# Attention with top-k and a mixture of experts on one core: two tiles of x turned by TensorE instead of by DMA

## The chip, the cores and the metric

The kernel runs on one core of a Trainium2 chip, in one launch. The metric is the device time in microseconds (us) of one execution. Five engines work side by side, each on its own list of instructions in order: TensorE (PE, matrix products), VectorE (DVE), ScalarE (ACT), GpSimd (POOL), and SyncE (SP), whose list here holds DMA issues only.

## The reference

Two batches, eight heads, 576 rows of queries and keys, 64 values a head. Attention keeps the 32 largest scores of each row; its output, one row of 512 values for each of 1152 rows, goes through four experts, each a product with w1, a ReLU and a product with w2, weighted by normalised probabilities.

```python
scores = scale * np.matmul(q, k.transpose(0, 1, 3, 2))
kth = np.partition(scores, -32, axis=-1)[..., -32:-31]
scores = np.where(scores >= kth, scores, -1e9)
attn = np.exp(scores - np.max(scores, axis=-1, keepdims=True))
attn = attn / (np.sum(attn, axis=-1, keepdims=True) + 1e-09)
x = np.matmul(attn, v)            # heads side by side: 1152 x 512
p = domain_probs / (domain_probs.sum(-1, keepdims=True) + 1e-09)
for e in range(4):
    h = np.maximum(x @ w1[e], 0.0)
    out += p[:, e:e + 1] * (h @ w2[e])
```

## The kernel before

**Tiles and units.** The 1152 rows are cut into ten tiles: of each batch four of 128 rows and one of 64. The half tile of the first batch comes first (here t0), then its four whole tiles (t1 the first of them), then the second batch. A unit is one head of a whole tile, or a pair of heads of a half tile, so 128 rows of 576 scores: units 0 to 3 are t0, 4 to 11 are t1, and so on to 71.

**Attention of a unit.** PE writes the scores into one of two score banks (L681; L636 for t0). DVE finds the 32 largest in four rounds of MAX8 (L694) with three MATCH_REPLACE8 between them (L696 for the first, L698). ACT takes the exp (L738). The mask sets all below the 32nd to zero: in the early units one DVE operation (L745), later one on ACT (L748) and POOL (L755). The mask reads the scores last, so only then is their bank free. In whole tiles ACT rounds the weights to fp16 (L764), POOL subtracts for the rest (L766, L768), and a DMA transpose on SP (L774) turns both; in t0 PE turns them in fp32 and ACT copies them out (L603, L604). PE multiplies with v (L805; L658 and L661 for t0). The keys are split in the same way, a POOL subtraction for each pair of heads, and turned by DMA transposes (L1141, tiles kt0 to kt7).

**x.** When four heads of a tile are summed, DVE divides them by their totals into x (L823, L825, L827, L829), 256 columns at a time. `emit_x_end` then rounds x to fp16 on ACT (L849, xhl), lets POOL subtract for the rest (L854), and turns both with one DMA transpose on SP (L857) into xt, which holds x turned, high and low parts, as the expert products want it. For t0, `emit_x_whole` turns x also in fp32 on PE (L838) and copies it out (L841), for the two experts whose weights are not yet split.

**Experts.** For each expert and each half of the 1024 hidden columns: first product (L922 to L924, three fp16 products of high and low parts; L897 in fp32), ReLU and split (L933, L940, L947 or L943), second product (L969; L960 in fp32), evacuation times the probability: ACT and POOL (L1014, L1019) or DVE alone (L1016). Weights are loaded by SP (L364), measured by a gram on PE (L528) whose diagonal DVE sums (L534) and PE adds up (L537), scaled by ACT (L558), rounded (L564), and their rest subtracted by POOL (L567).

**What sets the order.** Nothing is scheduled on the chip. Each step is a function, often a generator with several parts, entered with `at(...)`; `events` is drained in the order of the numbers in the table `ISSUE`, one tuple a step, one number a part, and each part's instructions are appended to the lists of their engines. An engine takes its list in order, so an instruction that waits holds back all behind it. Waits between engines follow from tiles written and read.

Of the kernel before, what the change touches and what calls it, by code (L numbers as in the profile page):

```python
# [8 lines left out]
F16 = mybir.dt.float16  # L9
# [37 lines left out]
NB = 'aaaaddddddaddaadaddddpdpdadppadpapppaaapppppadaappdaaaaaaapapaaaaaapapaa'  # L47
# [8 lines left out]
PC = ('pppp', 'pppp')  # L56

EVAC = ('ddpp', 'dppp', 'dppp', 'ddpd', 'dppp', 'dpdp', 'dddd', 'dddd', 'dddd', 'dddd')
# [177 lines left out]
def attn_moe_kernel(tc, q, k, v, probs, w1, w2, out):  # L236
# [69 lines left out]
    with tc.manual_schedule(engines={getattr(mybir.EngineType, x) for x in MANUAL}):  # L306
# [451 lines left out]
        def emit_a(u):  # L758
            if units[u][0] == tiles[0]:
                yield from emit_a_whole(u)  # L760
                return
# [8 lines left out]
        def emit_at(u):  # L770
            if units[u][0] == tiles[0]:
                return
# [529 lines left out]
```

## Time and profile before

| | |
|---|---|
| runs of the kernel before | 533.17, 534.58, 536.81 us (median 534.58) |
| profiled execution | 534.99 us, of which the span from first to last instruction is 533.2 us |
| busy in the span | PE 506.3, DVE 432.3, ACT 371.7, POOL 368.8 us |
| weight loads of PE | 377.8 us, beside the matmuls |
| mean granted clock of TensorE | 0.986 of full |

Busy time is an average over stages: PE's 95% does not say where the other 5% are, and DVE's 81% is nearly 100% in one half of the span and almost nothing at its end. A wait is put down to the releaser that came last; "idle before" in a row is the time in which the engine had nothing running ahead of that instruction.

### The profile page before, as it was taken

The page shows a single profiled execution, that of the slowest core. Times are in us where ns is not written, and L with a number is a line of the kernel's source. Part 1 is how long each engine was busy: PE and PEld are TensorE (multiplying, and loading weights), DVE is VectorE, ACT ScalarE, POOL GpSimd, SP SyncE. Part 2 cuts the span into 40 slices and gives each one's busy share as a digit, 9 for nine tenths or more (in the row PEclk, how much of TensorE's full clock was granted, in tenths as well). Part 3 has the DMA queues.
Part 4 walks back from the last instruction along what each step waited for, and adds up shares of the span by engine and source line. Part 5 has one row for each costly group of instructions (what it writes and reads, how often), then busy time and mean ns, then how long its engine had stood idle before and what let it go on. Part 6 is the DMA issues. An engine that isn't in the chain of part 4 may idle for free.

```text
span 533.2 us, 16075 instructions
## 1 busy us (share of the span) xinstructions
PE 506.3 (95%) x6594; PEld 377.8 (71%) x6594; DVE 432.3 (81%) x929; ACT 371.7 (70%) x612; POOL 368.8 (69%) x430
## 2 busy tenths in 40 slices
PE   7787788889999999999999999999999999999996
PEld 6576736477777777877777777777777866778576
DVE  4998989999999999999999999997879856910111
ACT  3899989998889887797777767775655644644121
POOL 0589989999999878678787875875565375454211
PEclk9996989999999999999999999999999999999999
DMA  8999969753465447457654652254232134221100
GB/s 189 316 295 358 219 183 234 164 87 55 90 110 121 103 95 116 94 115 114 125 120 70 97 104 59 57 95 76 57 64 57 30 75 54 21 47 43 33 23 11
DMA packets 142745, 58.33 MB, mean 109 GB/s; under 512 B 130064, under 2 KB 134416, under 8 KB 142672
## 3 DMA queue, kind: packets, MB, share of 16 engines
q1 hardware_dynamic: 138976, 54.43, 49.6%
q10 hardware_dynamic: 3696, 2.88, 1.8%
q8 instruction: 51, 0.84, 0.7%
q14 instruction: 22, 0.18, 0.1%
HBM read 25.45 MB, written 2.36 MB: 52 GB/s over the span
## 4 chain that ended last, share of the span: by engine, by line
PE 74%; DVE 16%; ACT 3%; POOL 3%; DMA 2%; issue 2%; SPq 0%; ACTq 0%; POOLq 0%
PE m L969 30%; PE m L922 10%; PE m L924 10%; PE m L923 10%; DVE m L694 7%; PE av L805 5%; PE ps L681 5%; DVE w L698 3%; DVE w L696 2%; POOL w L567 2%; DMA kraw<-in_k_dram 2%; DVE w L745 2%; PE m L528 1%; ACT w L564 1%; PE av L658 1%
## 5 line engine op out<-in xcount | busy, mean ns | idle before, releaser
L924 PE MATMUL m<-xt,w 128*128 128x128 f16 (+1 forms) x1216 | 191.2, 215 | 0.0
L969 PE MATMUL m<-w,h 128*128 128x512 f16 (+1 forms) x864 | 184.2, 379 | 0.1
L922 PE MATMUL m<-xt,w 128*128 128x128 f16 (+1 forms) x1056 | 171.0, 215 | 0.0
L923 PE MATMUL m<-xt,w 128*128 128x128 f16 (+1 forms) x1056 | 171.0, 215 | 0.0
L694 DVE MAX8 m<-w 128x8 f32<-128x576 f32 x216 | 161.9, 756 | 3.5
L969 PEld LDWEIGHTS <-h 128*128 128x128 f16 (+1 forms) x864 | 78.5, 99 | 85.9 <-DVE h L943 0.6
L924 PEld LDWEIGHTS <-w 128*128 128x128 f16 x1216 | 117.0, 98 | 0.0
L698 DVE MATCH_REPLACE8 w<-m,w 128x576 f32<-128x576 f32 x144 | 107.1, 744 | 0.0
L922 PEld LDWEIGHTS <-w 128*128 128x128 f16 x1056 | 101.9, 98 | 1.8 <-issue 0.4
L923 PEld LDWEIGHTS <-w 128*128 128x128 f16 x1056 | 101.8, 98 | 1.3
L947 POOL TENSOR_TENSOR h<-hf,h 128x512 f16<-128x512 f32 x55 | 63.7, 1159 | 53.8 <-ACT hf L940 29.1
L766 POOL TENSOR_TENSOR a<-w,a 128x512 f16<-128x512 f32 x68 | 78.9, 1160 | 17.6 <-ACT a L764 13.4
L755 POOL TENSOR_TENSOR w<-w,d 128x576 f32<-128x576 f32 x49 | 62.7, 1282 | 37.8 <-ACT d L752 27.8
L738 ACT ACTIVATE w<-ps,nb,es 128x576 f32<-128x576 f32 x68 | 56.3, 828 | 26.0 <-DVE m L694 23.7
L694 DVE MAX8 m<-ps 128x8 f32<-128x576 f32 x72 | 54.4, 756 | 16.2 <-PE ps L681 9.6
L764 ACT ACTIVATE a<-w 128x576 f16<-128x576 f32 x68 | 45.9, 679 | 22.7 <-POOL w L755 16.9
L933 ACT ACTIVATE h<-m 128x512 f16<-128x512 f32 x70 | 41.1, 591 | 23.8 <-PE m L924 23.1
L696 DVE MATCH_REPLACE8 w<-m,ps 128x576 f32<-128x576 f32 x72 | 53.9, 749 | 0.0
L1016 DVE SCALAR_TENSOR_TENSOR o<-m,pniw,o 128x512 f32<-128x512 f32 (+1 forms) x13 | 9.6, 742 | 48.7 <-PE m L969 23.0
L748 ACT ACTIVATE d<-ps,m 128x576 f32<-128x576 f32 x49 | 36.2, 739 | 18.2 <-DVE m L694 13.2
L940 ACT ACTIVATE hf<-m 128x512 f32<-128x512 f32 x55 | 32.5, 590 | 14.9 <-PE m L924 11.7
L805 PEld LDWEIGHTS <-at 128*128 128x128 f16 (+1 forms) x1008 | 35.1, 100 | 8.2 <-issue 4.7
(180 smaller groups left out, 818.5 us busy)
## 6 DMA issues: line engine op xcount, KB each, us to landing
w<-in_moe_w_dram SPq DMA_DIRECT2D x16, 1024.0 KB, 8.0
qraw<-in_q_dram SPq DMA_DIRECT2D x8, 256.0 KB, 4.0
qb<-qa SPq DMA_DIRECT2D x16, 128.0 KB, 3.7
out_dram<-o ACTq DMA_DIRECT2D x8, 256.0 KB, 2.2
at<-a SPq DMA_TRANSPOSE x68, 3.3
vraw<-in_v_dram SPq DMA_DIRECT2D x2, 512.0 KB, 8.3
nraw<-in_v_dram SPq DMA_DIRECT2D x4, 256.0 KB, 3.4
kraw<-in_k_dram SPq DMA_DIRECT2D x4, 256.0 KB, 2.9
```

The costliest lines, as they stand in the source:

```text
L694: DVE.max(m, s_t[u] if r == 0 else w_t[u])
L696: DVE.match_replace(rows2(w_t[u]), m, s_t[u], NEG)
L698: DVE.match_replace(w_t[u], m, w_t[u], NEG)
L738: ACT.activation(rows2(w_t[u]), s_t[u], AF.Exp, bias=nb, scale=es)
L755: POOL.tensor_tensor(w, w, g, op=OP.mult)
L766: POOL.tensor_tensor(a[:, 640:1152], w[:, 0:512], a[:, 0:512], op=OP.subtract)
L805: PE.matmul(o, lhsT=att[:, blk, ps], rhs=r, start=(i == 0), stop=(i == len(seq) - 1))
L922: PE.matmul(o, lhsT=HI[e, 0, c][:, fc], rhs=xs(0, c), start=(c == 0), stop=False)
L923: PE.matmul(o, lhsT=HI[e, 0, c][:, fc], rhs=xs(1, c), start=False, stop=False)
L924: PE.matmul(o, lhsT=LO[e, 0, c][:, fc], rhs=xs(0, c), start=False, stop=(c == 3))
L947: POOL.tensor_tensor(h[:, 1], hf, h[:, 0], op=OP.subtract)
L969: PE.matmul(y[z * 64:z * 64 + M, :], lhsT=h_t[es, qd][:, p // 2, h0:h0 + M], rhs=w, start=(fc == 0 and p == 0), stop=(fc == 7 and p == 2))
```

## The change

For the tiles listed in `X_TURN` (t0 and t1) x is no longer rounded, subtracted and sent through a DMA transpose. PE turns x in fp32 into a PSUM bank by products with the identity, ACT copies the bank to the high part in fp16, and DVE subtracts the high part from the bank for the low part. For t0 the turned x that `emit_x_whole` makes anyway is used, so no transposes are added there; for t1 `emit_x_turned` turns each half of x as soon as it stands. `emit_x_end` is not called for the two tiles. `A_TURN`, for the same with attention weights, is empty, and the function it would call (left out below) issues nothing. One evacuation goes from ACT and POOL to DVE (`EVAC`), one coefficient from POOL to DVE (`PC`), one bias from POOL to ACT (`NB`). The table `ISSUE` is new throughout; its first lines stand for it.

```diff
-NB = 'aaaaddddddaddaadaddddpdpdadppadpapppaaapppppadaappdaaaaaaapapaaaaaapapaa'
+NB = 'aaaaddddddaddaadaddddadpdadppadpapppaaapppppadaappdaaaaaaapapaaaaaapapaa'
-PC = ('pppp', 'pppp')
+PC = ('pppp', 'pppd')
+
+X_TURN = (0, 1)
+A_TURN = ()
-EVAC = ('ddpp', 'dppp', 'dppp', 'ddpd', 'dppp', 'dpdp', 'dddd', 'dddd', 'dddd', 'dddd')
+EVAC = ('ddpp', 'dppp', 'dppp', 'dddd', 'dppp', 'dpdp', 'dddd', 'dddd', 'dddd', 'dddd')
...
 ISSUE = [
-    (15,), (20,), (12,), (65,), (2, 3), (4, 5), (16, 19), (13, 14), (21, 27), (33,), (34, 37), (38, 43, 49, 74),
...
+        def emit_x_turned(t, half):
+            p = bank(ps_m1, "m1")[:, 0:256]
+            for c in range(2):
+                PE.transpose(p[:, c * 128:c * 128 + 128], x_t[t][:, half * 256 + c * 128:half * 256 + c * 128 + 128], ident)
+            yield
+            if half == 0:
+                xT_t[t] = xtp.tile([128, 8, 128], F16, tag="xt", name="xt")
+            hi, lo = (xT_t[t][:, i:i + 2].rearrange("p c n -> p (c n)") for i in (2 * half, 4 + 2 * half))
+            ACT.activation(hi, p, AF.Copy)
+            yield
+            DVE.tensor_tensor(lo, p, hi, op=OP.subtract)
+
         def emit_x_whole(t):
             p = bank(ps_m1, "m1")
             n = 256 if t[2] == 64 else 512
             for c in range(n // 128):
                 PE.transpose(p[:, c * 128:c * 128 + 128], x_t[t][:, c * 128:c * 128 + 128], ident)
+            if 0 in X_TURN:
+                yield
+                xT_t[t] = xtp.tile([128, 8, 128], F16, tag="xt", name="xt")
+                hi, lo = (xT_t[t][:, i:i + 2].rearrange("p c n -> p (c n)") for i in (0, 2))
+                ACT.activation(hi, p[:, 0:n], AF.Copy)
+                yield
+                DVE.tensor_tensor(lo, p[:, 0:n], hi, op=OP.subtract)
             yield
             xF[t] = hfp.tile([128, 512], F32, tag="hf", name="xf")[:, 0:n]
...
                 at(i + P["xh" + early], emit_x_half, t, (u - first_of[t]) // 4)
+                if ti and ti in X_TURN:
+                    at(i + P["xh" + early] + 1, emit_x_turned, t, (u - first_of[t]) // 4)
             if u == last_of[t]:
                 sfx = "_last" if ti == NT - 1 else early
-                emit_x_end(t, ti, [i + P[x + sfx] for x in ("sq", "tot", "hi", "lo")])
-                if t == tiles[0] and F32E:
+                if ti not in X_TURN:
+                    emit_x_end(t, ti, [i + P[x + sfx] for x in ("sq", "tot", "hi", "lo")])
+                if t == tiles[0]:
                     at(i + P["tot_first"], emit_x_whole, t)
```

**How the order moves, first place: DVE between the scores of unit 5 and of unit 6.** The w with the lower number is unit 4's in the first list, the higher one unit 5's; `ps0` in a MAX8 is a fresh bank of scores, here unit 6's, and L823 (L849 of the changed file) reads the sums of unit 3. Before:

```order
L823 TENSOR_SCALAR r_693<-av_471,ix_114 128x4
L694 MAX m_579<-w_605 128x8
L827 RECIPROCAL r_693<-r_693 128x4
L734 TENSOR_SCALAR nb_697<-m_579,es_559 128x1
L698 MATCH_REPLACE w_646<-m_639,w_646 128x576
L829 TENSOR_TENSOR x_692<-av_471,r_693 128x256
L694 MAX m_639<-w_646 128x8
L745 SCALAR_TENSOR_TENSOR w_605<-ps0_567,m_579,w_605 128x576
L698 MATCH_REPLACE w_646<-m_639,w_646 128x576
L694 MAX m_764<-ps0_759 128x8
L694 MAX m_639<-w_646 128x8
```

With the change:

```order
L698 MAX m_645<-w_653 128x8
L698 MAX m_584<-w_618 128x8
L702 MATCH_REPLACE w_653<-m_645,w_653 128x576
L849 TENSOR_SCALAR r_706<-av_482,ix_114 128x4
L698 MAX m_645<-w_653 128x8
L749 SCALAR_TENSOR_TENSOR w_618<-ps0_571,m_584,w_618 128x576
L538 SCALAR_TENSOR_TENSOR m1_710,gd_743<-m1_710,ident_111 128x128
L702 MATCH_REPLACE w_653<-m_645,w_653 128x576
L853 RECIPROCAL r_706<-r_706 128x4
L738 TENSOR_SCALAR nb_751<-m_645,es_611 128x1
L698 MAX m_759<-ps0_754 128x8
```

L823 went behind two more top-k operations; the division (L829, now L855) went behind unit 6's first MAX8, and the sum of the gram's diagonal (L534, now L538), which stood three rows below the first list, went ahead of it.

**Second place: SP's DMA issues from the load of w01 on.** `kt` are turned keys, `w` the raw weights of expert and layer, `khl0` and `xhl` the split keys and x. Before:

```order
L364 DMA w01_124<-in_moe_w2_dram 128x4x512
L1141 DMA_TRANSPOSE kt1_132<-khl0_144 128x5x128
L364 DMA w01_124<-in_moe_w2_dram 128x4x512
L1141 DMA_TRANSPOSE kt3_134<-khl0_144 128x5x128
L1141 DMA_TRANSPOSE kt2_133<-khl0_144 128x5x128
L1141 DMA_TRANSPOSE kt6_137<-khl0_144 128x5x128
L364 DMA w20_127<-in_moe_w1_dram 128x2x1024 x2
L364 DMA w11_126<-in_moe_w2_dram 128x4x512 x2
L1141 DMA_TRANSPOSE kt4_135<-khl0_144 128x5x128
L1141 DMA_TRANSPOSE kt5_136<-khl0_144 128x5x128
L857 DMA_TRANSPOSE xt_907<-xhl_741 128x4x128
L1141 DMA_TRANSPOSE kt7_138<-khl0_144 128x5x128
```

With the change:

```order
L368 DMA w01_124<-in_moe_w2_dram 128x4x512
L1186 DMA_TRANSPOSE kt2_133<-khl0_144 128x5x128
L368 DMA w01_124<-in_moe_w2_dram 128x4x512
L368 DMA w11_126<-in_moe_w2_dram 128x4x512
L368 DMA w20_127<-in_moe_w1_dram 128x2x1024
L1186 DMA_TRANSPOSE kt3_134<-khl0_144 128x5x128
L368 DMA w20_127<-in_moe_w1_dram 128x2x1024
L1186 DMA_TRANSPOSE kt7_138<-khl0_144 128x5x128
L368 DMA w11_126<-in_moe_w2_dram 128x4x512
L1186 DMA_TRANSPOSE kt6_137<-khl0_144 128x5x128
L1186 DMA_TRANSPOSE kt4_135<-khl0_144 128x5x128
L1186 DMA_TRANSPOSE kt5_136<-khl0_144 128x5x128
```

The transpose of xhl is gone, and of the four loads of w11 and w20, which went out together, the later half of each stands behind a key transpose (kt3, kt7). On POOL the subtraction for kt3 and kt7 went from the second of four key subtractions in a row to a place between the first two weight subtractions of w10.

**Third place: DVE just ahead of the scores of unit 16.** L745 (now L749) with `ps0_1593` (now `ps0_1590`) is the mask of unit 12, whose bank unit 16's scores take. Before:

```order
L694 MAX m_1598<-w_1631 128x8
L694 MAX m_1700<-ps0_1693 128x8
L298 TENSOR_SCALAR ws_117<-wpt_1407 128x1
L696 MATCH_REPLACE w_1742<-m_1700,ps0_1693 128x576
L745 SCALAR_TENSOR_TENSOR w_1631<-ps0_1593,m_1598,w_1631 128x576
L694 MAX m_1700<-w_1742 128x8
L534 SCALAR_TENSOR_TENSOR m1_1706,gd_1757<-m1_1706,ident_111 128x128
L698 MATCH_REPLACE w_1742<-m_1700,w_1742 128x576
L295 TENSOR_SCALAR wpt_1761<-m1_1706 128x1
L734 TENSOR_SCALAR nb_1764<-m_1700,es_1191 128x1
```

With the change:

```order
L855 TENSOR_TENSOR x_1437<-av_1558,r_1658 128x256
L702 MATCH_REPLACE w_1614<-m_1611,w_1614 128x576
L870 TENSOR_TENSOR xt_1546<-m1_1542,xt_1546 128x256
L698 MAX m_1611<-w_1614 128x8
L698 MAX m_1702<-ps0_1697 128x8
L870 TENSOR_TENSOR xt_1546<-m1_1693,xt_1546 128x256
L700 MATCH_REPLACE w_1715<-m_1702,ps0_1697 128x576
L538 SCALAR_TENSOR_TENSOR m1_1720,gd_1753<-m1_1720,ident_111 128x128
L698 MAX m_1702<-w_1715 128x8
L749 SCALAR_TENSOR_TENSOR w_1614<-ps0_1590,m_1611,w_1614 128x576
```

The two subtractions of t1 (L870 of the changed file) are new, L534 (now L538) went from behind this mask to ahead of it, and the mask of unit 14 went ahead of the division of x, out of this list.

## Rows read from the trace of the kernel before

**Rows 1.** Windows by stage; columns: stretch, us, busy us (instructions) by engine, PEclk, DMA, GB/s.
```profile
core 0: us, PE busy (x) PEld busy (x) DVE busy (x) ACT busy (x) POOL busy (x), PEclk, DMA share, GB/s
0.00:40.00 40.00, 31.68 (x378) 24.65 (x380) 31.83 (x81) 29.32 (x47) 19.07 (x30) 1.00 1.02 267
40.00:80.00 40.00, 32.12 (x424) 22.87 (x420) 35.86 (x88) 36.41 (x43) 35.98 (x34) 0.83 0.88 253
80.00:111.00 31.00, 25.95 (x300) 16.11 (x297) 30.72 (x77) 29.28 (x35) 30.43 (x32) 1.00 0.88 179
111.00:160.00 49.00, 47.39 (x644) 36.73 (x642) 48.62 (x105) 43.95 (x67) 47.73 (x49) 1.00 0.53 88
160.00:370.00 210.00, 209.99 (x2623) 158.27 (x2621) 202.03 (x421) 158.61 (x294) 160.35 (x206) 1.00 0.53 98
```

**Rows 2.** Timeline of PE: start us, us, engine, line, operation [idle before, what ended it].
```profile
39.76 0.69 PE L658 MATMUL av<-vraw,at 128*64 128x64 f32 x16 [0.53 <-ACT at L603]
...
41.94 3.59 PE L528 MATMUL m<-w 128*128 128x128 bf16 x32
45.33 0.63 PE L838 MATMUL m<-ident,x 128*128 128x128 f32 x2
...
105.98 0.30 PE L681 MATMUL ps<-kt,qa 128*128 128x288 f16 x1 [0.91 <-DVE w L745]
...
106.48 2.00 PE L528 MATMUL m<-w 128*128 128x128 bf16 x32
110.08 0.38 PE L537 MATMUL m<-gd,ones 128*128 128x1 f32 x2 [1.60 <-DVE m L534]
...
110.81 0.22 PE L922 MATMUL m<-xt,wx 128*128 128x128 f16 x1
...
154.86 0.28 PE L681 MATMUL ps<-kt,qa 128*128 128x288 f16 x1 [0.64 <-ACT w L738]
```

**Rows 3.** Timeline of DVE, 40 to 47 us.
```profile
42.05 0.22 DVE L823 TENSOR_SCALAR r<-av,ix 128x4 f32<-128x4 f32 x1 [1.20 <-PE av L661]
...
43.76 0.42 DVE L829 TENSOR_TENSOR x<-av,r 128x256 f32<-128x256 f32 x1
44.09 0.76 DVE L694 MAX8 m<-w 128x8 f32<-128x576 f32 x1
...
46.96 0.77 DVE L694 MAX8 m<-ps 128x8 f32<-128x576 f32 x1 [0.67 <-PE ps L681]
```

**Rows 4.** Timeline of ACT, 38 to 47 us.
```profile
39.13 0.58 ACT L603 ACTIVATE at<-m 128x512 f32<-128x512 f32 x1
...
41.80 1.06 ACT L564 ACTIVATE w<-w 128x1024 f16<-128x1024 f32 x1
```

**Rows 5.** Timeline of DVE, 108 to 110 us.
```profile
108.29 0.81 DVE L745 SCALAR_TENSOR_TENSOR w<-ps,m,w 128x576 f32<-128x576 f32 x1
...
109.68 0.28 DVE L534 SCALAR_TENSOR_TENSOR m<-m,ident 128x128 f32<-128x128 f32 x1
```

**Rows 6.** Timeline of SP, the queue of DMA issues.
```profile
37.91 2.86 SPq L364 DMA_DIRECT2D w<-in_moe_w_dram  x4
...
106.84 1.26 SPq L857 DMA_TRANSPOSE xt<-xhl  x1
```

**Rows 7.** Tile xt: time from issue to landing of its transposes.
```profile
DMA to landing us min/median/max: 2.4/3.4/4.8
```

**Rows 8.** Line 364, weight loads issued from 37 to 41 us: time to landing.
```profile
DMA to landing us min/median/max: 5.9/8.7/12.0
```

**Rows 9.** Window of 42 to 44 us, columns as in rows 1.
```profile
42.00:44.00 2.00, 2.00 (x21) 2.00 (x21) 1.95 (x7) 1.69 (x2) 1.65 (x2) 0.50 1.02 410
```

**Rows 10.** Tile x: duration ns min/median/max, first and last start us, forms.
```profile
L849 ACT ACTIVATE xhl<-x x10: 416/629/631, 44.2 to 500.1; 128x512 f16<-128x512 f32 x8, 128x256 f16<-128x256 f32 x2
L854 POOL TENSOR_TENSOR xhl<-x,xhl x10: 670/1155/1180, 47.7 to 500.6; 128x512 f16<-128x512 f32 x8, 128x256 f16<-128x256 f32 x2
```

**Rows 11.** Line 1016, columns as in rows 10.
```profile
L1016 DVE SCALAR_TENSOR_TENSOR o<-m,pniw,o x13: 732/742/751, 246.3 to 518.9; 128x512 f32<-128x512 f32 x12, 64x512 f32<-64x512 f32 x1
```

More of the change, by code (lines that the diff above doesn't have):

```diff
@@ L756, in emit_mask, with emit_a_turned @@
                 s_give(("d", u))
+        def emit_a_turned(u):
+            t, x = units[u]
+            w = w_t.pop(u)
+            p0 = bank(ps_m1, "m1")
+            if (t, x // 4) not in av_t:
+                av_t[t, x // 4] = bank(ps_av, "av")
+            p1 = av_t[t, x // 4][:, 384:512]
+            for c in range(4):
+                PE.transpose(p0[:, c * 128:c * 128 + 128], w[:, c * 128:c * 128 + 128], ident)
+            PE.transpose(p1, w[:, 448:576], ident)
+            PE.transpose(p1[0:64], w[:, 512:576], ident)
+            yield
+            at_t[u] = tt = atp.tile([128, 9, 128], F16, tag="at", name="at")
+            ACT.activation(tt[:, 0:4].rearrange("p c n -> p (c n)"), p0, AF.Copy)
+            ACT.activation(tt[:, 4], p1, AF.Copy)
+            yield
+            DVE.tensor_tensor(tt[:, 5:9].rearrange("p c n -> p (c n)"), p0, tt[:, 0:4].rearrange("p c n -> p (c n)"), op=OP.subtract)
+            DVE.tensor_tensor(tt[64:128, 4], p1[64:128], tt[64:128, 4], op=OP.subtract)
         def emit_a(u):
@@ L760, in emit_a @@
                 yield from emit_a_whole(u)
+                return
+            if u in A_TURN:
+                yield from emit_a_turned(u)
                 return
@@ L770, in emit_at @@
         def emit_at(u):
-            if units[u][0] == tiles[0]:
+            if units[u][0] == tiles[0] or u in A_TURN:
                 return
@@ L838, in emit_x_whole @@
                 PE.transpose(p[:, c * 128:c * 128 + 128], x_t[t][:, c * 128:c * 128 + 128], ident)
+            if 0 in X_TURN:
+                yield
+                xT_t[t] = xtp.tile([128, 8, 128], F16, tag="xt", name="xt")
+                hi, lo = (xT_t[t][:, i:i + 2].rearrange("p c n -> p (c n)") for i in (0, 2))
+                ACT.activation(hi, p[:, 0:n], AF.Copy)
+                yield
+                DVE.tensor_tensor(lo, p[:, 0:n], hi, op=OP.subtract)
             yield
```

318 rows, old and new, of the table ISSUE are left out of this document.

## The prediction

> **What bounds the kernel now.** I read the table by stages first [rows 1]. TensorE (PE) is busy without a gap from 160 to 370 us and has 1.61 us of idle from 111 to 160 (49.00 - 47.39). Ahead of that it idles 7.88 us from 40 to 80 and 5.05 us from 80 to 111, and there VectorE (DVE) is the full one: 30.72 of 31.00 us from 80 to 111. The reader should see two regimes: up to about 111 us the top-k on DVE hands out the score banks and PE waits for it; from there on PE has expert matmuls in stock and is the bound to the end. So the time is "when PE gets its stock" plus PE's work after that. The second view is PE's own order of time [rows 2]. The stock arrives at 110.81, where the first matmul of the first whole tile (t1) starts. It does not start on x: PE stands first at a gram sum (1.60 us of idle up to 110.08, until DVE's L534 is done) and then at the scores of unit 16, and only behind those come the t1 matmuls. The third view is DVE from 108 to 110 us [rows 5]: the mask of unit 12, a MAX8 between, then the L534 for which PE stood.
>
> The DMA transpose that the change removes had its turn: issued at 106.84 [rows 6], with a median landing of 3.4 us [rows 7] it is there at 110.2, against 110.81. It is hidden by 0.6 us in the median, and at the longest landing of this tile name, 4.8 us, it would be 0.8 us late. So removing it is worth 0 to 0.8 us, and I take 0, because PE names L534 and not a DMA as what it waited for. What the transposes did elsewhere has to pay for the change.
>
> **The change part by part, against the profiled run: 534.99 us with a span of 533.2, 0.41 above the median of the three runs (534.58).**
>
> The extra DVE work. Three subtractions that read PSUM, 128x256 each, come onto DVE ahead of unit 16's scores: one for the half tile t0, two for t1. Otherwise DVE's list up to that point holds the same operations as before. The nearest row is L829, 128x256 out of PSUM: 0.42 us, and the next operation starts 0.33 us after it [rows 3]. Three cost 1.0 to 1.3 us on an engine that is full; **+1.0**.
>
> The stretch from 40 to 47 us. DVE idles 1.20 us for the attention sums of unit 3 and then 0.67 us for the scores of unit 6 [rows 3]. In the new order the L823 on those sums stands two top-k operations later, so the first gap can close; the second is set by PE: sums of unit 3, gram of w01, scores of unit 6, in this order. PE loses 0.53 us ahead of unit 3's sums, waiting for the copy L603 [rows 2], which begins at 39.13 [rows 4]; in the new order one L564 copy (1.06 us [rows 4]) stands behind it instead of ahead. And the two transposes of x (0.63 us [rows 2]) no longer stand between gram and scores. That brings unit 6 about 1.0 us forward. The L534 for w01 now stands ahead of unit 6's first MAX8 and makes DVE wait for the end of the gram, which keeps the gain from being more. **-1.0**, bounds 0 and -1.9 (both DVE gaps).
>
> The order just ahead of the stock. Before, DVE ran mask, MAX8, L534 (from 108.29 to past 109.68 [rows 5]), and PE took the sum and then the scores. Now it runs L534, MAX8, mask: the sum is no longer waited for, and the scores of unit 16 are released by the last of the same three. Nothing is won but the sum's own turn, part of its 0.38 us [rows 2], **-0.2**. Queued behind that wait are unit 16's scores and all of t1's matmuls.
>
> TensorE's new work. Four more transposes of 128x128 fp32. At half clock two take 0.63 us [rows 2]; so four are 0.6 to 1.3 us. The second pair stands ahead of unit 15's scores, where PE idled 0.91 us (at 105.98); the first pair stands in a stretch with 5.05 us of idle. **0** while that cover holds, +1.3 if it doesn't.
>
> ScalarE and POOL. ACT loses an x copy of 0.42 us and one of 0.63 us [rows 10], and gains three of 128x256 out of PSUM, for which the 0.42 us one is the nearest row: +0.2 beside other work, nothing. POOL loses 0.67 and 1.15 us [rows 10]; it is full from 80 to 160 (30.43 of 31.00, 47.73 of 49.00 [rows 1]). Of PE's 1.61 us of idle after 111 the largest piece, 0.64 us before 154.86, ends on an exp on ACT [rows 2]; the ACT chain there runs behind POOL's. I take that one piece as gone, **-0.6**; ends 0 and -1.6.
>
> The rest. One evacuation of the fourth tile goes from ACT and POOL to DVE at 0.74 us [rows 11]; it falls in 160 to 370, where DVE idles 7.97 us against PE's 0.01 [rows 1]: 0. One bias of a single column goes from POOL to ACT and one coefficient from POOL to DVE, 0. After 111 the order of expert matmuls, sums and scores is shuffled by a place or two with the same work: 0. SP loses two transposes and gets its weight loads in another order; that is a rival below.
>
> Sum: 1.0 - 1.0 - 0.2 - 0.6 = -0.8, so 534.99 - 0.8 = **534.2 us**.
>
> [...]
>
> **Rivals.**
>
> *All DVE gaps close* (chance 0.2). Against the forecast, DVE idles 4.14 us from 40 to 80 and 0.28 us from 80 to 111 [rows 1]. If the new order closes these, and PE's 1.61 us after 111 as well, the time is 534.99 + 1.0 - 0.2 - 4.4 - 1.6 = 529.8; with about half of it, 532. For it: two of the gaps are waits for PE at half clock, and a full clock alone would give the gram's 1.6 us back. [...]
>
> *TensorE falls to half clock near 105 us* (chance 0.08). The second pair stands between fp32 matmuls and a gram. If the clock falls there, the gram and what follows cost twice: 1.6 us for the gram, and then PE is already the bound, so the t1 matmuls pay in full. All falls from 40 to 80 us together cost 40 x (1 - 0.83) = 6.8 us of full clock [rows 1]; half of that, 3.4, for one fall here. 534.2 + 3.4 = 537.6, slower than before. It decides if the granted clock falls below 1 between 105 and 115 us.
>
> *The second halves of w20 and w11 come late* (chance 0.15). Before, four loads went out together at 37.91 [rows 6] and landed 5.9 to 12.0 us later, median 8.7 [rows 8]. Now the second half of each stands on SP behind a key transpose (kt3, kt7), and kt3 waits for POOL's key subtraction, which has moved behind a weight subtraction. By POOL's pace that is near 41 us; the loads would go out near 44 and 46, and at 8.7 us land near 52.5 and 55. The grams of w20 and w11 stand in PE ahead of unit 8's scores, so DVE then starves with them: about +1.9 us at the median, +5.2 at 12.0 us. The time is 536.1, and 539.4 at the worst. For it: nothing else can slip in between, PE is in order. Against it: with fewer loads at a time each should land sooner. It decides if the later half lands after 53 us.
>
> *The turn does nothing that counts* is the forecast's own core: neither removed transpose ended last.
>
> **How the numbers follow.** Forecast and its neighbourhood (533 to 536) 0.52; gaps close (529.8 to 533) 0.2; late weights (536 to 539.4) 0.15; half clock 0.08 (near 537.6); 0.05 for a wait that I don't see in the shuffled stages. The range 530.0 to 538.5 leaves out the far ends of these, under 2 in 10. A measurement of this kernel tells about 1%, 5.3 us, from no change: faster than 529.2 needs every gap gone and a little more, 0.08; slower than 539.9 needs the longest landings or two mishaps together, 0.08; the rest, 0.84, is within 1%.
>
> **What would show it.** The first t1 matmul starts at 110.0 to 111.0 us; no idle of 1.6 us before the gram sum just ahead of it; DVE's idle from 40 to 80 near 3 us instead of 4.14, and its idle at 42 us gone, with a wait of up to 1 us for the gram of w01 in its place; PE idle from 111 to 160 near 1 us; granted clock 1.00 from 80 us on. The forecast is wrong if the first t1 matmul starts before 108 or after 113 us, if PE idles in 160 to 470, or if the grams of w20 and w11 wait for a DMA.

## The result and the profile of the changed kernel

The changed kernel takes 539.67 us (median of six runs; 538.17 to 540.02), the kernel before 534.97 us beside it (six runs, 533.17 to 536.81). The ratio that goes with these runs is 1.0068 with the interval 1.0044 to 1.0092; it is not the quotient of the two medians, which is 1.0088. The forecast was 534.2 us, a little faster, in a range of 530.0 to 538.5 us: the kernel became slower, and the time lies above the range. The profiled execution has a span of 538.1 us, 4.9 longer than before. One run of old_order_behind_16 below (1034.43 us) and one of the kernel before beside it (542.63 us) were slow ones, and the figures here leave them out.

The windows by stage, with the columns of [rows 1]:

```profile
0.00:40.00 40.00, 32.24 (x330) 23.99 (x330) 29.18 (x76) 27.48 (x46) 16.56 (x28) 0.97 1.04 277
40.00:80.00 40.00, 32.66 (x441) 25.06 (x442) 35.46 (x85) 33.37 (x38) 33.27 (x30) 0.74 0.82 223
80.00:111.00 31.00, 27.41 (x311) 16.66 (x306) 30.90 (x77) 29.28 (x40) 30.29 (x34) 1.00 0.80 178
111.00:160.00 49.00, 45.84 (x612) 35.90 (x610) 48.39 (x109) 46.16 (x67) 47.52 (x47) 1.00 0.51 93
160.00:370.00 210.00, 209.47 (x2593) 156.56 (x2592) 201.98 (x419) 158.38 (x294) 158.79 (x201) 1.00 0.52 96
```

Against [rows 1], DVE has done 2.65 us less work in the first 40 us (29.18 for 31.83), ahead of the stretch from 40 us that the prediction costed; the granted clock from 40 to 80 fell from 0.83 to 0.74; and PE idles 0.53 us from 160 to 370, where it had idled 0.01.

The timeline of PE in the same kernel, columns as in [rows 2]; L640 is the scores of unit 0, L648 the weight transposes of unit 3, L685 scores, L662 attention sums, L532 grams:

```profile
8.49 1.88 PE L640 MATMUL ps<-kf,qf 64*64 64x288 f32 x8
...
37.24 1.11 PE L648 MATMUL m<-ident,w 128*128 128x128 f32 x4 [0.86 <-DVE w L749]
...
38.93 0.42 PE L685 MATMUL ps<-kt,qa 128*128 128x288 f16 x1
...
40.01 1.12 PE L662 MATMUL av<-vraw,at 128*64 128x64 f32 x16
...
45.44 3.59 PE L532 MATMUL m<-w 128*128 128x128 bf16 x32
48.83 0.44 PE L685 MATMUL ps<-kt,qa 128*128 128x288 f16 x1
...
54.12 0.42 PE L685 MATMUL ps<-kt,qa 128*128 128x288 f16 x1 [3.91 <-DVE wpt L299]
```

The same places in the kernel before (L636 is the scores of unit 0, L681 those of unit 5, L644 the weight transposes of unit 3):

```profile
7.48 1.19 PE L636 MATMUL ps<-kf,qf 64*64 64x288 f32 x8
...
35.93 0.28 PE L681 MATMUL ps<-kt,qa 128*128 128x288 f16 x1
...
36.42 0.60 PE L644 MATMUL m<-ident,w 128*128 128x128 f32 x4
```

Two things differ. In the durations, from 37.24 us on matmuls take half as long again to nearly twice as long as the same ones at full clock (16 sums in 1.12 us for the 0.69 of [rows 2]): the granted clock from 37 to 58 us is 0.51, near the 0.50 of [rows 9], and was 0.76 before. The first row is the same at the start: 8 score matmuls in 1.88 us, where before they took 1.19. In the order, the scores of unit 5 stood ahead of unit 3's transposes and now stand behind them and behind their wait. What DVE makes of it, columns as in [rows 3]:

```profile
10.41 0.77 DVE L698 MAX8 m<-ps 128x8 f32<-128x576 f32 x1 [2.33 <-PE ps L640]
...
40.11 0.77 DVE L698 MAX8 m<-ps 128x8 f32<-128x576 f32 x1 [1.40 <-PE ps L685]
...
45.56 0.22 DVE L849 TENSOR_SCALAR r<-av,ix 128x4 f32<-128x4 f32 x1 [0.52 <-PE av L665]
...
49.07 0.30 DVE L538 SCALAR_TENSOR_TENSOR m<-m,ident 128x128 f32<-128x128 f32 x1 [1.90 <-PE m L532]
...
110.66 0.41 DVE L870 TENSOR_TENSOR xt<-m,xt 128x256 f16<-128x256 f32 x1
```

Between the first MAX8 of unit 4 and that of unit 6, three waits for PE, 3.82 us in all, stand where two stood before with 1.87 us [rows 3]; DVE's own work there is the same (11.53 us, before 11.54). The last row is one of the new subtractions. Unit by unit, the first MAX8 is later than in the profile before ("late" in what follows) by 1.70 us (unit 0), 0.99 (unit 3), 1.29 (unit 4), 2.79 (unit 5), 3.24 (unit 6), and 3.43 (unit 16): only 0.19 us are added between units 6 and 16. The first expert matmul of t1 starts 3.14 us late, at 113.95. Then PE:

```profile
112.11 0.38 PE L541 MATMUL m<-gd,ones 128*128 128x1 f32 x2 [0.64 <-DVE m L538]
113.45 0.30 PE L685 MATMUL ps<-kt,qa 128*128 128x288 f16 x1 [0.95 <-DVE w L749]
...
113.95 0.22 PE L967 MATMUL m<-xt,w 128*128 128x128 f16 x1
...
120.14 0.30 PE L685 MATMUL ps<-kt,qa 128*128 128x288 f16 x1 [0.67 <-DVE w L749]
...
121.77 0.22 PE L967 MATMUL m<-xt,wx 128*128 128x128 f16 x1 [0.53 <-ACT h L978]
...
154.61 0.28 PE L685 MATMUL ps<-kt,qa 128*128 128x288 f16 x1 [0.27 <-ACT d L752]
...
191.17 0.59 PE L1014 MATMUL m<-w,h 128*128 128x512 f16 x2 [0.33 <-DVE kps L302]
...
375.58 0.22 PE L967 MATMUL m<-xt,wx 128*128 128x128 f16 x1 [0.79 <-ACT hf L985]
```

From there to the end it takes 424.15 us (538.1 - 113.95), before 422.39 (533.2 - 110.81): another 1.76. So the 4.9 us are 3.14 ahead of the stock, all of which stood at unit 6 already (3.24), and 1.76 behind it. Of these 1.76, idle time of PE makes 1.17 (6.84 us for 5.67); for the other 0.59 PE is busy longer with the same 5512 matmuls, and no run names the cause. The first 50 us behind the first t1 matmul hold no more idle time than before (1.56 us, before 1.61): the waits of 0.67 and 0.53 us stand in place of others. From there to 370 us there are 0.53 us in place of 0.01, of which the row at 191.17 is 0.33, and from 370 to 500 us 0.79 in place of 0, the row at 375.58; the stretches before and behind these give back some 0.15.

Each run has its own mean granted clock: 0.971 to 0.984 in the six runs of the changed kernel, 0.978 in the profiled one. So none of them ran at full clock throughout, but where it was lower is known for the profiled one alone.

### The profile page after: what moved, and what is told of

Same layout as the page of the kernel before. It is cut to its first block, busy times and chain, and to the rows that moved or that the text cites. A ratio compares the mean times of both kernels' runs of the same rounds, so it can differ in the third digit from the quotient of the medians.

```text
span 538.1 us, 16050 instructions
## 1 busy us (share of the span) xinstructions
PE 511.0 (95%) x6598; PEld 381.6 (71%) x6598; DVE 434.9 (81%) x934; ACT 370.6 (69%) x613; POOL 365.2 (68%) x425
## 4 chain that ended last, share of the span: by engine, by line
PE 67%; DVE 22%; issue 3%; POOL 3%; ACT 2%; DMA 1%; SPq 0%; ACTq 0%; POOLq 0%; DVEq 0%
PE m L1014 27%; DVE m L698 10%; PE m L967 10%; PE m L969 9%; PE m L968 9%; DVE w L702 5%; PE av L831 4%; PE ps L685 4%; DVE w L700 3%; DVE w L749 2%; POOL w L759 1%; DMA kraw<-in_k_dram 1%; PE av L662 1%; DMA qraw<-in_q_dram 1%; PE m L532 1%
## 5 line engine op out<-in xcount | busy, mean ns | idle before, releaser
L685 PE MATMUL ps<-kt,qa 128*128 128x288 f16 x128 | 35.0, 293 | 9.5 <-DVE w L749 5.2
```

The costliest lines, as they stand in the source:

```text
L685: PE.matmul(ps[:, 0:288], lhsT=src[:, x, :], rhs=kt[x].rearrange("p c n -> p (c n)")[:, ks], start=(j == 0), stop=(j == 1))
```

## The experiments

Each is compared with runs of the kernel before on the same chip; the ratio is what counts, since that kernel's own median lay between 535.8 and 536.5 us there. Here too the ratio is not simply the quotient of two medians. Where `ISSUE` is written anew the file is longer, and line numbers differ. Of a move in the order the diff shows the steps, not the numbers.

**Is it the order of the first 50 us, or the turn?** Two kernels exchange the head (the order up to the scores of unit 6), two separate the turn from the order.

```diff
 # after_head_of_before: the changed kernel
-new order up to the scores of unit 6
+old order up to the scores of unit 6
 new order behind
```

> The changed kernel with all steps up to and including the scores of unit 6 issued in the old order (some 45 us of the program), the rest in the new order, x of t0 and t1 still turned by TensorE. Theory A (the new order of the first 50 us makes the loss; the first top-k of unit 6 is 3.24 us late there and the lateness stays from then on): the first top-k of unit 6 near 47.0 us, the time back to 535 to 536 us. Rival B (the turn makes it: three more subtractions on VectorE, four more transposes on TensorE): the time stays at 538.5 to 540.

537.78 us, ratio 1.0047 (1.0023 to 1.0071): part of the way back, not all. In its profile unit 6 is 2.62 us late, but 2.52 of that stood at unit 4 already, in an order that is the old one up to there; from unit 4 to unit 6 it takes 13.51 us, as before (13.41).

```diff
 # before_head_of_after: the kernel before
-old order up to the scores of unit 6
+new order up to the scores of unit 6
 old order behind
```

> The mirror: the kernel before, x by DMA transposes, with the steps up to and including the scores of unit 6 in the new order, the rest in the old. Theory A: 538 to 540 us, first top-k of unit 6 near 50 us, half clock on TensorE from about 37 to 57 us. Rival B: 535 us.

537.38 us, 1.0036 (1.0010 to 1.0061): between the two forecasts. The two effects, 0.36% for the new head and 0.47% for the new rest, make 0.83% where 0.68% was measured, within the intervals. Theory A holds for about half of the loss.

```diff
 # turn_alone: old order
-x_hi, x_lo, xt by DMA for t0 and t1
+emit_x_whole with its split for t0; emit_x_turned for t1, its first half behind the scores of unit 12
```

> The old order with nothing but the turn: x of t0 and t1 turned by TensorE and split by ScalarE and VectorE where the rounding, subtraction and DMA transpose stood. (The three single-letter flips of EVAC, PC and NB are in too.) Theory A: within 0.7 us of the kernel before, 534.5 to 535.7. Rival B: 538 to 540. My own term for the three subtractions, +1.0 less what POOL and ScalarE are relieved of, gives 535 to 536.

536.98 us, 1.0025 (0.9993 to 1.0056), scattered from 533.98 to 539.61. Not 538 to 540 by its ratio, yet too scattered for a price. Its profile shows where scatter can come from. PE, with the list of the kernel before:

```profile
12.31 1.39 PE L2036 MATMUL m<-ident,kraw 128*128 128x128 f32 x5 [0.23 <-DMA kraw<-in_k_dram]
13.62 2.13 PE L2062 MATMUL ps<-kf,qf 64*64 64x288 f32 x8
```

The same transposes and scores took 0.83 and 1.19 us in the profile before. PE had idled 1.70 and twice some 0.2 us just ahead, and unit 4 is 2.92 us late with no instruction changed up to there. The 25 runs of the kernel before in this comparison fall in two groups, twelve from 532.58 to 534.92 and thirteen from 536.53 to 538.14, with none between. Their mean granted clocks part in the same way: 0.987 to 0.994 in the lower group, 0.978 to 0.984 in the upper. In the next comparison, on another chip, the 30 runs from 532.83 to 539.01 show no such gap, but the clock goes with the time again: 0.984 to 0.994 in the 17 up to 536.57 us, 0.974 to 0.980 in the 13 above. The profile that I predicted from (534.99 us, clock 0.986) is one of the faster kind.

```diff
 # turn_undone: the changed kernel
-X_TURN = (0, 1)
+X_TURN = ()          # x_hi, x_lo and the DMA transpose issued where the turn's parts stood
```

> The new order with x of t0 and t1 rounded, subtracted and sent through DMA transposes again, issued where the turn's parts stood. Theory A: 539 to 540 us, as the changed kernel. Rival B: 535 to 536.

543.74 us, 1.0162 (1.0120 to 1.0204): slower still. In the new order the turn isn't the cost: it saves 4.1 us by the medians and 5.0 by the ratios, against DMA transposes placed as I placed them. From the first expert matmul of t1 to the end it takes 427.18 us here, 3.0 more than in the changed kernel. PE of this kernel:

```profile
43.18 2.01 PE L1956 MATMUL m<-w 128*128 128x128 bf16 x32
...
114.02 0.22 PE L2391 MATMUL m<-xt,w 128*128 128x128 f16 x1 [0.74 <-DMA xt<-xhl]
...
121.65 0.30 PE L2109 MATMUL ps<-kt,qa 128*128 128x288 f16 x1 [2.10 <-DVE w L2173]
```

ScalarE of it:

```profile
113.03 1.06 ACT L1992 ACTIVATE w<-w 128x1024 f16<-128x1024 f32 x1 [2.07 <-POOL w L1995]
```

Now the transposed x ends last, by 0.74 us, and a mask behind an exp on ScalarE holds PE 2.10 us; ScalarE itself had stood 2.07 us for POOL, which has x's subtraction to do again (1.16 us, just ahead of the L1995 that ScalarE waits for). The first row is worth as much: the head is that of the changed kernel, word for word, and here the gram took 2.01 us and unit 6 came only 0.51 us late, though unit 4 was 2.32 late. With the clock at full for most of it (0.92 from 37 to 58 us) the new order makes up time in that stretch; in the profile of the changed kernel, at half clock, it loses 1.95 us there.

**Is it TensorE's clock?**

```diff
+def fill(n): n matmuls of ones by ones, 128x128, into the bank of the attention sums
 # before_filled
 scores of unit 0;            +fill(20)
 gram of k;                   +fill(8)
 sum of k's gram;             +fill(16)
 first gram of a weight;      +fill(20)
 gram of v;                   +fill(10)
```

> The kernel before with TensorE kept busy in its idle pieces of the first 26 us: 74 spare matmuls (ones by ones, 128x128, into the bank of the attention sums, read by nobody) behind the scores of unit 0 (20), the gram of k (8), its sum (16), the first gram of a weight (20) and the gram of v (10). Two profiles with the old head show the transposes and scores of units 1 and 2 at half rate from about 12 us on (8 score matmuls in 2.13 us against 1.19 us) and unit 4's top-k 2.5 to 2.9 us later than the profile before. Theory C (the kernel before has two levels, near 534 and near 537 us, as TensorE's clock falls or doesn't in the first 25 us): the upper level is gone or rare, median 533.5 to 534.8, 8 score matmuls at 1.19 us for all of units 0 to 3. Rival D (the levels come from elsewhere, the arrival of k or q say): as before, both levels, median 535 to 537.

533.08 us, 0.9949 (0.9925 to 0.9973): faster than the kernel before, with seven of ten runs between 532.58 and 533.20. Theory C holds: the runs above are few (three at 534.5 to 535.6), and the mean granted clock is 0.984 to 0.996, beside 0.974 to 0.994 without the fills. In its profile, one of those three, the scores of units 0, 1 and 3 take 1.19 us each, and the gram of w01 still runs at half clock:

```profile
39.51 0.79 PE L664 MATMUL av<-vraw,at 128*64 128x64 f32 x16 [0.39 <-ACT at L607]
...
41.89 3.59 PE L530 MATMUL m<-w 128*128 128x128 bf16 x32
```

```diff
 # after_filled: the changed kernel
 gram of k;                   +fill(30)
 first gram of a weight;      +fill(28)
```

> The changed kernel with 58 spare matmuls of the same kind, 30 behind the gram of k, where TensorE waits 2.05 us, and 28 behind the first gram of a weight, where it waits 1.94 us. Theory C: the half rate between 12 and 24 us goes, some 1 to 2 us sooner at unit 4, 537.5 to 538.7 us. Rival D: 539 to 540.

539.53 us, 1.0077 (1.0046 to 1.0107): a miss, no gain. In its profile one fall came ahead of the first fill (scores of unit 1 in 2.19 us at 12.43, the fill at 16.01), and a second one at 39 us, long after the last (clock 0.95 over the first 37 us, 0.67 from 37 to 58).

```diff
 # scores5_first: the changed kernel
 attention sums of unit 1
+scores of unit 5
 weight transposes of unit 3
-scores of unit 5
 attention sums of units 2 and 3
```

> The changed kernel with one move: the scores of unit 5 ahead of the weight transposes of unit 3, as the old order has them; these wait 0.86 us for unit 3's mask. Theory A: VectorE's idle piece of 1.40 us ahead of unit 5's first MAX8 goes, the attention sums of units 2 and 3 start about 1 us sooner, and the time falls by 1 to 1.4 us, to 538.2 to 538.7. Rival (the lateness comes from TensorE's half clock and the later sums alone): unit 6 no sooner, 539.7.

536.79 us, 1.0013 (0.9984 to 1.0043): more than forecast. In its profile the 1.40 us of idle ahead of unit 5 is gone and unit 5 is 0.04 us late:

```profile
35.97 0.28 PE L2107 MATMUL ps<-kt,qa 128*128 128x288 f16 x1 [0.86 <-DVE w L2171]
...
37.49 1.12 PE L2084 MATMUL av<-vraw,at 128*64 128x64 f32 x16
...
42.91 3.59 PE L1954 MATMUL m<-w 128*128 128x128 bf16 x32
```

From unit 4 to unit 6 it takes 14.10 us here and 15.36 in the changed kernel: 1.26 for the move, as forecast. The fall came all the same, at 37.49 (16 sums in 1.12 us for 0.69; clock 0.67 from 37 to 58 us). The other 1.3 us between the two profiles lie ahead of unit 4, 1.29 us late in that one, where the scores of unit 0 took 1.88 us for 1.19; in this one units 1 to 3 are 0.6 us early. Whether the ten runs gained their rest in the same way isn't shown; their clocks, 0.970 to 0.990, reach higher than the 0.971 to 0.984 of the changed kernel.

The next two put spare matmuls into the waits ahead of the fall.

```diff
 # before_filled_more: before_filled, and
 attention sums of unit 2;    +fill(10)
 scores of unit 6;            +fill(22)
 # scores5_filled: scores5_first, and
 scores of unit 0;            +fill(14)
 gram of k;                   +fill(12)
 first gram of a weight;      +fill(18)
 attention sums of unit 1;    +fill(12)
```

> before_filled with 10 more spare matmuls behind the attention sums of unit 2 (ahead of a wait of 0.39 us and of the half clock from 40 to 47 us) and 22 behind the scores of unit 6 (ahead of a wait of 2.63 us). If they hold the clock: the gram at 41.9 us in 2.0 us in place of 3.59, unit 6 about 1.5 us sooner, 531.5 to 532.5 us. If not: the sums of unit 3 come some 0.3 us later, 533 to 533.5.

> The changed kernel with the scores of unit 5 ahead of the weight transposes of unit 3, and spare matmuls behind the scores of unit 0 (14), the gram of k (12), the first gram of a weight (18) and the attention sums of unit 1 (12, where TensorE waits 0.86 us ahead of the half clock at 37 us). If what is left of the loss is the clock in the first 50 us: 533.5 to 535, narrow. If 1.8 us of it lies behind 111 us, as the profiles so far say: 534.5 to 536, no nearer to before_filled than 1.4 us.

before_filled_more: 532.59 us, 0.9935 (0.9913 to 0.9958), the fastest kernel here, ahead of both. PE of it:

```profile
39.31 0.73 PE L1076 MATMUL m<-ones 128*128 128x128 bf16 x10
...
41.63 2.01 PE L531 MATMUL m<-w 128*128 128x128 bf16 x32
...
45.30 0.28 PE L688 MATMUL ps<-kt,qa 128*128 128x288 f16 x1 [0.94 <-DVE w L752]
```

With ten spare matmuls in a wait that was 0.39 us long without them, the gram takes 2.01 us in place of 3.59, and the scores of unit 6 wait for DVE, no longer DVE for them. One profile each can't show that the ten did it: turn_alone_filled below, without them, has the gram in 2.01 us too. The clocks of all runs point the same way, though: 0.993 to 0.999 in the six of before_filled_more, 0.984 to 0.996 in the ten of before_filled.

scores5_filled: 536.19 us, 1.0005 (0.9985 to 1.0025). In its profile the gram takes 2.01 us as well (clock 0.84 from 37 to 58 us), unit 6 is 1.23 us earlier than in the kernel before, and yet scores5_filled is 3.1 us behind before_filled by their medians. In the profiles it is 1.9 us, and their first expert matmuls of t1 start at 109.72 and 109.64. So the clock is not all; what is left lies behind.

The distance from unit 4's first MAX8 to unit 6's, one profile each, puts the clock and the order side by side:

| order of that stretch | gram of w01 in 3.59 us | gram in 2.01 us |
|---|---|---|
| old | 13.41, 13.47, 13.51, 13.61 | 12.59 (32 fills), 11.93 |
| new | 15.36, 14.91, 14.32 | 11.60, 11.59 |
| new, scores of unit 5 first | 14.10 | 11.25, 11.25 (12 fills each) |

Every entry of the right column is below every entry of the left. Of the two new-order entries there, 11.60 (turn_undone) and 11.59 (old_order_behind_16, below), a part is slack made up, since unit 4 itself is 2.3 and 4.3 us late in those profiles; neither kernel has a fill, so the new order can run that stretch with the gram in 2.01 us without one.

**What is the turn's own price?**

```diff
 # turn_alone_filled: turn_alone with the five fills of before_filled
```

> The turn alone in the old order, with the 74 spare matmuls of before_filled, which take away most of the scatter of the first 25 us. It gives the turn's own price. If my term for the three PSUM subtractions holds (+1.0 us, relief of POOL and ScalarE to be taken off): 533.1 to 534.1 us, by the median of before_filled (533.08). If the turn costs more in the old order, where it stands badly (behind the scores of unit 12, so that the first expert matmul of t1 comes later): 534.5 to 536.

534.48 us, 0.9972 (0.9946 to 0.9998), 1.4 us above before_filled by the medians and 1.2 by the ratios, between the two forecasts; its runs still scatter (532.46 to 539.17), and the two intervals overlap, so the price can't be told from nothing. In its profile the first expert matmul of t1 starts at 109.58, in before_filled's at 109.64.

**What is lost behind 111 us?** From the first expert matmul of t1 to the end the profiles with the old order there take 422.39 (before), 422.42, 422.58, 422.62, 422.67 and 423.06 us, those with the new order and the turn 424.15 (the changed kernel), 424.22, 424.27, 424.60 and 424.88. Profiles of one order there differ by up to 0.7 us.

```diff
 # old_order_behind_16: the changed kernel
 new order up to the scores of unit 16
-new order behind
+old order behind
```

> The changed kernel, turn and all, in the new order up to the scores of unit 16 and in the old order behind them. Theory E (the new order behind 111 us costs 1.1 to 1.5 us by itself: TensorE idles 2.59 us there from the first expert matmul of t1 on, against 1.5 us before): 538.2 to 538.6, no idle piece of 0.79 us near 375 us. Rival (all of the loss lies ahead of unit 16): 539.7.

539.05 us, 1.0063 (1.0032 to 1.0093): inconclusive. The piece at 375 us is gone, and from unit 20 to the end 0.2 us are lost (4.63 us late, then 4.8), where the changed kernel loses 2.0 (2.89, then 4.9). But the seam between the two orders itself costs: unit 16 is 2.55 us late, unit 18 5.38, and from the first expert matmul of t1 to the end it takes 424.94 us, no less than the new order.

```diff
 # scores5_filled_out: scores5_filled, and on ScalarE's list, fifth tile's end
-output DMA (evac, last part)
 ReLU and split of the next tile's first expert: rounding, copy, rounding
+output DMA (evac, last part)
```

> scores5_filled with one more move, far from the first 50 us: the DMA issue that writes the fifth tile's output stands on ScalarE's list behind the ReLU and split of the next tile's first expert (a rounding, a copy, a rounding) in place of ahead of them. With the new order ScalarE stands 1.77 us at this issue, until POOL's sum is done, and TensorE then waits 0.79 us near 372 us for the bank that the copy behind it frees. Theory E (such single waits make the 1.8 us behind 111 us): no idle piece of 0.79 us at 372, and 424.1 to 424.2 us from the first expert matmul of t1 to the end (three profiles of the new order) become 423.3 to 423.5. Rival: the piece moves to a later wait, 424.1. The median, 536.19 for scores5_filled, falls by 0.8 at most, which its scatter of 2.7 us hardly shows; the profile decides.

535.03 us, 0.9977 (0.9955 to 0.9999). ScalarE and PE of scores5_filled around the place:

```profile
370.01 0.34 ACTq L2497 DMA_DIRECT2D out_dram<-o  x1
370.39 0.60 ACT L2407 ACTIVATE h<-m 128x512 f16<-128x512 f32 x1 [1.77 <-POOL o L2493]
...
372.10 0.22 PE L2396 MATMUL m<-xt,wx 128*128 128x128 f16 x1 [0.79 <-ACT hf L2414]
```

ScalarE of scores5_filled_out:

```profile
366.90 0.68 ACT L2488 ACTIVATE yf<-m,pniw 128x512 f32<-128x512 f32 x1
367.47 0.59 ACT L2407 ACTIVATE h<-m 128x512 f16<-128x512 f32 x1
367.94 0.69 ACT L2219 ACTIVATE a<-w 128x576 f16<-128x576 f32 x1
368.96 0.60 ACT L2414 ACTIVATE hf<-m 128x512 f32<-128x512 f32 x1 [0.32 <-POOL o L2493]
369.81 0.60 ACT L2407 ACTIVATE h<-m 128x512 f16<-128x512 f32 x1 [0.25 <-PE m L2398]
369.81 0.34 ACTq L2497 DMA_DIRECT2D out_dram<-o  x1
```

The roundings no longer stand behind the DMA issue, and PE has no idle piece there: from 370 to 500 us it idles 0.00 us, where scores5_filled idles 0.79, so the piece did not turn up later. The stretch behind the first expert matmul falls from 424.88 to 424.10. Of the rest, a wait near 147 us grew by 0.18 (1.28 to 1.46) and PE is busy 0.14 less, which nearly cancel, so that the 0.78 us are the whole piece; it is one profile each. The number expected, 423.3 to 423.5, was missed, and 424.1 is the rival's number, but not by the rival's mechanism: the wait near 147 us, for turned attention weights, stands in all three filled kernels of the new order (1.28 us in after_filled at 152.88) and not in the three profiles without fills (424.15, 424.22, 424.27) that the forecast started from.

## Why the prediction was wrong, by its steps

**The extra DVE work, +1.0**, was sized right for one instruction (0.41 us, as [rows 3] had it). From unit 6 to unit 16, where all three subtractions stand, the profile takes 64.69 us for 64.50: DVE is busy 0.64 us longer and idle 0.45 less. It isn't what made the loss.

**The stretch from 40 to 47 us, -1.0**, is the first step that failed, and for two reasons. I read how the order moves inside it, on DVE, and not what feeds it. PE's list ahead of it had changed as well: the scores of unit 5 went behind unit 3's weight transposes, which wait 0.86 us for a mask. And I took the clock of the profile before as given. [rows 9] had shown half clock from 42 to 44 us; the profile of the changed kernel has it from 37 to 58 (0.51). With the gram in 2.01 us the sign of my term may be right (11.6 us from unit 4 to 6 against 11.9 and 12.6 in the old order, a part of it slack); with the gram in 3.59 us the new order takes 14.3 to 15.4, the old 13.4 to 13.6. The measured term is +1.95 in place of -1.0, all of it waits of DVE for PE; 1.26 came back with the scores of unit 5 alone (scores5_first).

**A quarter of the profiled loss was in no term:** the first 12 us. Unit 4 is 1.29 us late, because the scores of unit 0 came 1.70 us late: 0.27 for a later load of q, the rest in slower matmuls (k's five transposes 1.41 us for 1.19, ten of ones by ones 1.25 for 0.73, the scores 1.88 for 1.19). That isn't the order: scores5_first, with the same order there, has units 1 to 3 0.6 us early.

**The order ahead of the stock, -0.2**: nothing. PE waits 0.64 us for the sum and 0.95 us for the scores, 1.59 together, as much as the 1.60 of [rows 2]. **TensorE's new work, 0**: the cover held, since PE still idles 3.59 us from 80 to 111 us.

**ACT and POOL, -0.6**: the piece of 0.64 us [rows 2] shrank to 0.27, but other waits took its place, and PE idles 1.56 us in the 50 us behind its first t1 matmul, before 1.61: nothing. **"The rest", 0** for the shuffled order behind 111 us, is the other failed step: +1.76, as 0.52 us of new idle time up to 370 us and 0.79 behind, on a PE that had been without a gap there, and 0.59 us in which it is busy longer. The 0.79 was taken away and did not come back elsewhere; the others weren't tried.

**The signs.** Two of those that were to show the forecast wrong came: the first t1 matmul starts at 113.95, later than 113, and PE idles between 160 and 470 us.

**The rivals.** Half clock was on my list, with 3.4 us as its price, and 0.08 as its chance: near 105 us, where I thought a new pair of transposes might bring it. It came at 37 us, ahead of the first transposes of x (55.05), and the stretch from unit 4 to 6 lost 1.95 us with it. That the turn's transposes make a fall was my estimate, and no run here shows it: from 105 to 115 us the clock of the changed kernel reads 1.00. Late second halves of w20 and w11 did not count: issued at 44.12 and 45.99, they landed within 5.6 and 7.5 us, the later at 53.5, just behind the 53 that was to decide, and their grams at 55.48 wait for no DMA. That the turn does nothing that counts was read off the old order; in the new order a DMA transpose is late (0.74 us in turn_undone).

**The base.** The sum started from one profile, 534.99 us, of a kernel whose runs spread from 532.6 to 539.7 us with their clock, and that profile was of the faster kind. Against the later medians of that kernel (535.8 to 536.5) the loss is nearer 3 us than 5.

**What stays open:** where the clock of the changed kernel falls in its other runs, since only one profile shows a place; their mean clocks (0.971 to 0.984, around the profile's 0.978) say only that each of them lost some. Why the clock falls at 37 us in one profile of this order and not in another (turn_undone); the 0.59 us of longer work behind 111 us; and the turn's price in the old order.

## What to carry to other kernels

Read PE's durations against the same instruction elsewhere before costing any move: where they differ as the 3.59 and 2.01 us of the gram of w01 do here, the clock is a term of its own, and with it a stretch of some 13 us changed by 1 us and more. Compare runs by their mean granted clock before comparing their times. Here 106 spare matmuls in waits of the first 50 us gave 0.65% (interval 0.42 to 0.87), more than either version of the order; the 58 of after_filled, behind one fall and long before the next, gave nothing (1.0077, the changed kernel 1.0068). And when an order is written anew, a shuffle on an engine that has no gap should not be put at 0: here it brought waits of 0.33 and 0.79 us, and without the 0.79 the stretch was 0.78 us shorter (scores5_filled_out).

## What the runs showed of the hardware

The granted clock from 7 to 11 us reads 1.00 in the changed kernel's windows, while the same 8 score matmuls take 1.88 us there and 1.19 us in the kernel before: there the duration shows the slow rate and the row doesn't. The rate in the first 25 us differs between executions of one list of instructions: it gave 1.19 us (the kernel before) and 2.13 us (turn_alone) for the scores of unit 1. Where the slow durations stand differs too: in turn_alone at 12.31 and 13.62 us (five transposes of k in 1.39 us for 0.83, then those scores), in the changed kernel ahead of that (the 1.88 us at 8.49), and its scores of unit 1 take 1.19 us at 12.55. How clock and time go together is shown by the 25 runs of the kernel before beside turn_alone: a mean clock of 0.987 or more goes with 532.6 to 534.9 us, 0.984 or less with 536.5 to 538.1.
